# Taking the numerator of a linear-attention block two token tiles at a time, with other matmuls between it and the output projection

## The chip, the cores and the metric

The kernel runs on one core of a Trainium2 chip. Five engines work side by side and meet only at semaphores: TensorE (PE in the profile; PEld is its loading of weights), VectorE (DVE), ScalarE (ACT), GpSimd (POOL) and SyncE (SP), which issues most DMAs. Each engine takes its instructions strictly in the order in which they stand in its queue. The metric is the device time of one execution in microseconds (us).

## What is computed

One block of a network on 2048 tokens with 512 channels, in float32: linear attention with a learned feature map, then an MLP over the tokens.

```python
# attention, 32 heads of 16 channels, on the layer-normed x
phi_q = concat([softmax(pq), softmax(-pq)])     # pq = q @ w_phi, per head; phi_k likewise
kv  = einsum("bhsf,bhsd->bhfd", phi_k, v)
z   = einsum("bhsf->bhf", phi_k)
num = einsum("bhqf,bhfd->bhqd", phi_q, kv)
den = einsum("bhqf,bhf->bhq", phi_q, z) + 1e-6
h   = x + (num / den) @ wo
# token MLP on the layer-normed h
u   = gelu(einsum("bsd,sf->bdf", layernorm(h), w1) + b1)
out = h + (einsum("bdf,fs->bds", u, w2) + b2).transpose
```

## The kernel before, in words

The tokens lie in 16 tiles of 128. A first stage makes k, v and the sums kv and z. A second stage, the loop at L630, goes over the token tiles and makes num, the projection by wo, h and its normed copy. A last stage does the rest of the MLP: the matmuls with w1 that are still to do, gelu, and the matmuls with w2 (L764). Every large matmul is made of three: both factors are split into a high and a low part (`oh`/`ol`, `hs` with two halves, `whi`/`wlo`), and `mm3` (L60 to L64) adds high by high, high by low and low by high.

The loop of the second stage has 19 rounds, called `it`. What round `it` issues, by helper:

- `s_num(it-1)` (L536): 16 small matmuls, each on 64 rows and 32 columns of the array, give the numerator of one tile in PSUM (`tn`); ScalarE copies its high part to `oh` (L547), VectorE makes `ol` (`s_ol`, L552).
- `s_wo(it-2)` (L554): 12 matmuls of 512 columns into the one buffer `po`. VectorE then adds x (`s_h`, L568) and the result h goes out by DMA.
- `s_tr(it)` (L521): 8 transposes of the weighted features `eq` into `tn`, which has a single buffer of two PSUM banks and is shared with `s_num`; ScalarE copies them to `pht` (L527).
- `s_pq(it+1)` (L459, GpSimd): weights `eq` by one over the denominator. That comes from `s_ez` (L440, GpSimd, for tile it+3) and `s_den` (L444, VectorE, for tile it+2; its first step, L451, reduces `ez`).
- `s_moments(it-3)`, `s_rstd(it-3)`, `s_hn(it-3)` (L571 to L586): the layer norm of h on ScalarE and GpSimd. `s_hn` ends with the copy `hn` (ScalarE), the high part of `hs` (ScalarE, L57) and its low part (GpSimd, L58).
- Fills: `fill(p)` (L616) does 12 / 2 = 6 matmuls for one of the two column blocks of w1, p = 0 or p = 1, and one token tile whose `hs` is there. From round 6 on there are two of them in each round. The other fills, five more column blocks, follow after the loop. `fill_load` fetches the pieces of w1, ScalarE copies `whi` (L604), and `flush` (L593) makes `wlo` on VectorE (L596).

Inside the loop the order on PE, VectorE, ScalarE and GpSimd is the order of the program text: the loop stands in a manual schedule (L419) that is closed at L672. Behind it a scheduler orders the instructions. SyncE's queue is ordered by the scheduler throughout. Pools decide how many buffers a tile has; a new tile in a full pool waits until the old one was read for the last time.

Of the kernel before, what the change touches and what calls it, by code (L numbers as in the profile page):

```python
# [9 lines left out]
F32 = mybir.dt.float32  # L10
F32R = mybir.dt.float32r
AF = mybir.ActivationFunctionType
# [5 lines left out]
P = 128  # L18
S, D, H, DH, F = 2048, 512, 32, 16, 1792
NT = S // P  # L20
KD = D // P
NF = F // P
NG = 8
# [2 lines left out]
V_NOT = (0, 1, 11)  # L26
SUMS = 8
LAG = 4
WARM = 9
EPS = 1e-5  # L30

# [2 lines left out]
def block_kernel(ctx: ExitStack, tc: tile.TileContext, x, xT, wT, phic, wo, w1, b1, w2, b2,  # L34
                 kvmask, ident_in, out):
    nc = tc.nc
# [31 lines left out]
    ps_q = ctx.enter_context(tc.tile_pool(name="ps_q", bufs=2, space=PSUM, side="right"))  # L68
# [5 lines left out]
    kvB = wqp.tile([P, 2, P], F32, name="kvB")  # L74
# [87 lines left out]
    def turns(*lists):  # L162

        return [ops[i] for i in range(max(map(len, lists))) for ops in lists if i < len(ops)]

    def run(*lists):
        for op in turns(*lists):
            op()
# [4 lines left out]
    def heads(e):  # L173
        return e.rearrange("p g (a d) -> p (g a) d", d=DH)
# [43 lines left out]
    with tc.tile_pool(name="prep", bufs=1) as prep:  # L218
# [67 lines left out]
        warm = ps_k.tile([P, P], F32, name="pk_ps", tag="pk_ps")  # L286
        for _ in range(WARM):
            nc.tensor.matmul(warm, ones, ones, start=True, stop=True)
# [91 lines left out]
    def q_sums(lag):  # L380
        n = q["sum"]
        if n < min(NT, q["exp"] - lag + NT * (q["exp"] == NT)):
            q["sum"] += 1
            return q_sum(n)
        return []
# [54 lines left out]
    def s_ez(t):  # L440
        EZ[t] = az.tile([P, NG, P], F32, name="ez")
        nc.gpsimd.tensor_mul(EZ[t], EQ[t], zB)  # L442

    def s_den(t):  # L444


        tz = az.tile([P, NPR, 2, 2], F32, name="tz")
        den = az.tile([P, NPR, 2], F32, name="den")
        W[t] = az.tile([P, NPR, 2, 2], F32, name="w", bufs=3)
        other = SQ[t]  # L450
        return [lambda: nc.vector.reduce_sum(tz.rearrange("p g c h -> p (g c h)"), heads(EZ[t]), axis=AX.X),  # L451
                lambda: nc.vector.scalar_tensor_tensor(tz[:, :, 0], other[:, :, 1], 1e-6, tz[:, :, 0],
                                                       op0=ALU.mult, op1=ALU.add),
                lambda: nc.vector.tensor_mul(tz, other, tz),
                lambda: nc.vector.reduce_sum(den, tz.rearrange("p g c h -> p g h c"), axis=AX.X),
                lambda: nc.vector.reciprocal(den, den),
                lambda: nc.vector.tensor_mul(W[t], other, den.unsqueeze(2).to_broadcast([P, NPR, 2, 2]))]  # L457

    def s_pq(t):  # L459
        nc.gpsimd.tensor_mul(heads(EQ[t]), heads(EQ[t]), W[t].rearrange("p g c h -> p (g c h)").unsqueeze(2).to_broadcast([P, 2 * H, DH]))  # L460
# [51 lines left out]
    ps_f = ctx.enter_context(tc.tile_pool(name="ps_f", bufs=2, space=PSUM, reuse_waits="tile"))  # L512
# [3 lines left out]
    ak = a2.enter_context(tc.tile_pool(name="ak", bufs=2, reuse_waits="tile"))  # L516
    ps_t = a2.enter_context(tc.tile_pool(name="ps_t", bufs=1, space=PSUM, reuse_waits="tile"))
    ps_o = a2.enter_context(tc.tile_pool(name="ps_o", bufs=1, space=PSUM, reuse_waits="tile"))
    HN, HT, PHT, OS, PO, VE = {}, {}, {}, {}, {}, {}

    def s_tr(t):  # L521
        PHT[t] = ak.tile([P, NG, P], F32, name="pht")
        ptr = ps_t.tile([P, 2, 4, P], F32, name="tn")
        for g in range(NG):
            nc.tensor.transpose(ptr[:, g // 4, g % 4, :], EQ[t][:, g, :], ident)  # L525
        for half in range(2):
            nc.scalar.activation(PHT[t][:, half * 4:half * 4 + 4, :], ptr[:, half], AF.Copy)  # L527

    def s_kv():

# [2 lines left out]
            nc.tensor.transpose(pt[:, b, :], kvS[:, 2 * b:2 * b + 2, :].rearrange("p n f -> p (n f)"), ident)  # L533
        nc.scalar.activation(kvB, pt, AF.Copy)

    def s_num(t):  # L536

        pn = ps_t.tile([P, 2, 4, P], F32, name="tn")[:, :, 0:2]
        for b in range(2):
            for c in range(4):  # L540
                for r in range(2):
                    rows, cols = slice(64 * r, 64 * r + 64), slice(32 * c, 32 * c + 32)
                    nc.tensor.matmul(pn[cols, r, b, :], kvB[rows, b, cols], PHT[t][rows, 4 * b + c, :],  # L543
                                     start=True, stop=True, skip_group_check=True)
        oh = ak.tile([P, 2, 2, P], F32R, name="oh")
        ol = ak.tile([P, 2, 2, P], F32R, name="ol")
        nc.scalar.activation(oh, pn, AF.Copy)  # L547
        OS[t] = oh, ol, pn

    def s_ol(t):  # L550
        oh, ol, pn = OS[t]
        return [lambda: nc.vector.tensor_sub(ol, pn, oh)]  # L552

    def s_wo(t):  # L554
        oh, ol, _ = OS.pop(t)
        PO[t] = po = ps_o.tile([P, D], F32, name="po")
        for j in range(4):
            mm3(po, oh[:, j // 2, j % 2, :], ol[:, j // 2, j % 2, :], woh[:, j, :], wol[:, j, :], j == 0, j == 3)

    def s_x(t):  # L560
        HT[t] = ak.tile([P, D], F32, name="h", bufs=4)
        nc.sync.dma_start(HT[t], x[t * P:(t + 1) * P, :])

    def s_h(t):

        h = HT[t]
        VE[t] = ak.tile([P, 4], F32, name="ve2", bufs=3)
        nc.vector.scalar_tensor_tensor(h, PO.pop(t), 1.0, h, op0=ALU.mult, op1=ALU.add, accum_out=VE[t][:, 2:3])  # L568
        nc.sync.dma_start(out[t * P:(t + 1) * P, :], h)

    def s_moments(t):  # L571

        junk = ak.tile([P, D], F32, name="hj", bufs=1)
        nc.scalar.activation(VE[t][:, 1:2], VE[t][:, 2:3], AF.Copy, scale=-1.0 / D)
        nc.scalar.activation(junk, HT[t], AF.Square, bias=VE[t][:, 1:2], accum_out=VE[t][:, 3:4])
        nc.scalar.activation(VE[t][:, 0:1], VE[t][:, 3:4], AF.Identity, scale=(1.0 + EPS) / D, bias=eps2)

    def s_rstd(t):
        nc.gpsimd.tensor_tensor(r2[:, t:t + 1], VE[t][:, 0:1], mhalf[:, :1], op=ALU.pow)
        nc.gpsimd.tensor_mul(VE[t][:, 1:2], VE[t][:, 1:2], r2[:, t:t + 1])  # L580

    def s_hn(t):
        hn = ak.tile([P, D], F32, name="hn")
        nc.scalar.activation(hn, HT[t], AF.Identity, scale=r2[:, t:t + 1], bias=VE[t][:, 1:2])
        HN[t] = big.tile([P, 2, D], F32R, name="hs", tag="big")
        split(HN[t][:, 0], HN[t][:, 1], hn, nc.gpsimd)  # L586
# [4 lines left out]
    LATER = []  # L591

    def flush():  # L593
        while LATER:
            wl_, raw, wh_ = LATER.pop(0)
            LO.append(nc.vector.tensor_sub(wl_, raw, wh_).ins)  # L596
# [11 lines left out]
    PU, WI, LO = {}, {}, []  # L608
    FN, FL = [0] * (NF // 2), [0] * (NF // 2)

    def fill_load(p):
        if FL[p] < NT:
            WI[p, FL[p]] = stream(w1v, FL[p], 2, p * 256, 256)
            FL[p] += 2

    def fill(p, pool=None):  # L616

        t = FN[p]
        FN[p] = t + 1
        if FL[p] <= t:  # L620
            fill_load(p)
            flush()
        if t == 0:
            PU[p] = [pool.tile([P, D], F32, name="pu", tag="pu") for _ in range(2)]
        a, b = WI[p, t - t % 2]
        for c in range(2):
            mm3(PU[p][c], a[:, t % 2, c * P:(c + 1) * P], b[:, t % 2, c * P:(c + 1) * P],
                HN[t][:, 0], HN[t][:, 1], t == 0, t == NT - 1)

    for it in range(NT + 3):  # L630
        if 0 <= it < NT:
            s_x(it)
        if 0 <= it - 1 < NT:
            s_num(it - 1)
        if 0 <= it - 3 < NT:
            s_moments(it - 3)
        if 0 <= it - 2 < NT:
            s_wo(it - 2)
        if it == 1:
            run(q_logits(0))  # L640
            q_mm()
        if 0 <= it < NT:
            s_tr(it)
        if it == 0:
            s_kv()
        if 0 <= it + 1 < NT:
            s_pq(it + 1)
        if 0 <= it - 3 < NT:
            s_rstd(it - 3)
        lead(it, 1)  # L650
        den = s_den(it + 2) if it + 2 < NT else []
        ql = q_logits(1)
        ops = turns((s_ol(it - 1) if 0 <= it - 1 < NT else []) + ql + (q_sums(0) if it > 0 else []), den)

        at = 7 if ql else 3
        ops[at:at] = [flush]
        ops[3:3] = [lambda: s_h(it - 2)] if 0 <= it - 2 < NT else []
        run(ops)
        if it > 0:
            negate()  # L660
        if 0 <= it - 3 < NT:
            s_hn(it - 3)
        if FN[0] <= it - LAG:
            fill(0, ps_f)
        for _ in range(2):
            if q["logits"] == NT and FN[1] <= it - LAG:
                fill(1, ps_q)
        for p in range(2):
            if it >= LAG - 2 and FL[p] <= FN[p] + 1:
                fill_load(p)  # L670
    flush()
    ms.close()  # L672
# [102 lines left out]
    for n, (sp, p) in enumerate(STEPS):  # L775
        t = 2 * sp
# [93 lines left out]
```

## Time and profile before

| what | us |
|---|---|
| median of 3 timed runs | 530.6 |
| lowest, highest | 530.51, 530.87 |
| the profiled execution | 530.48 |
| its span, first to last instruction | 528.7 |
| start of the numerator of tile 0 (round 1), of tile 15 (round 16), from the span's start | 146.28, 256.88 |

A profile describes one execution. It gives each instruction's start and duration, and groups and merges them: a row of the timeline is start, duration, engine, line, operation, output and inputs, shape and how many were merged. Several matmuls are in flight at a time, so their durations overlap; the distance from one start to the next is what a matmul costs a full PE. L numbers are lines of the kernel before.

In the changed kernel, lines from L26 on stand at least one line lower.

### The profile page before, as it was taken

How to read it: one execution, taken by the hardware profiler on the slowest of the kernel's cores; microseconds unless marked ns; L12 is line 12 of the kernel's file. 1: busy time of each engine (PE TensorE's matmuls, PEld its weight loads, DVE VectorE, ACT ScalarE, POOL GpSimd, SP SyncE). 2: the span in 40 equal slices, each digit the busy share in tenths (PEclk: the TensorE clock that was granted, in tenths of full speed). 3: DMA queues.
4: the chain of work that ended last, by engine and by line, in shares of the span. 5: the costliest groups of instructions: out<-in, count | busy, mean ns of one | idle time of the engine just before them, and what ended most of it. 6: DMA issues, size and time to landing. Idle time of an engine off the chain costs nothing.

```text
span 528.7 us, 9887 instructions
## 1 busy us (share of the span) xinstructions
PE 521.3 (99%) x3872; PEld 450.0 (85%) x3872; DVE 378.8 (72%) x680; ACT 272.2 (51%) x460; POOL 230.9 (44%) x190
## 2 busy tenths in 40 slices
PE   8999999999999999999999999999999999999996
PEld 7888888887877777777888888888899999999996
DVE  6993999876899888773426424835668878987784
ACT  6998833525237776676657323526444243343340
POOL 2589699876999988985335000000001101101110
PEclk9999999999999999999999999999999999999999
DMA  8634300012303223333255333542015466535631
GB/s 315 199 116 119 90 33 21 1 45 97 102 1 100 73 89 119 121 121 120 81 178 161 104 97 98 161 119 81 20 41 113 134 152 151 128 122 121 160 73 48
DMA packets 45487, 55.85 MB, mean 106 GB/s; under 512 B 3968, under 2 KB 33024, under 8 KB 45440
## 3 DMA queue, kind: packets, MB, share of 16 engines
q1 hardware_dynamic: 43136, 51.38, 30.7%
q0 software_dynamic: 2016, 3.67, 5.2%
q8 instruction: 30, 0.49, 0.4%
q10 hardware_dynamic: 288, 0.17, 0.1%
q14 instruction: 17, 0.14, 0.1%
HBM read 46.81 MB, written 8.39 MB: 104 GB/s over the span
## 4 chain that ended last, share of the span: by engine, by line
PE 95%; DVE 3%; DMA 1%; ACT 0%; issue 0%; DVEq 0%
PE py L764 26%; PE pu L62 12%; PE pu L64 12%; PE pu L63 12%; PE po L62 3%; PE pv L63 3%; PE pv L64 3%; PE pv L62 3%; PE po L63 3%; PE po L64 3%; PE tn L525 3%; PE pk_ps L62 2%; PE pk_ps L64 2%; PE pk_ps L63 2%; PE tn L543 2%; PE kvp L207 2%
## 5 line engine op out<-in xcount | busy, mean ns | idle before, releaser
L802 POOL DMA_DIRECT2D out<-ot x14 | 12.5, 1000 | 211.9 <-DVE ot L800 211.9
L764 PE MATMUL py<-uf,whi 128*128 128x256 f32 x560 | 96.2, 283 | 0.0
L57 ACT ACTIVATE whi<-wraw 128x1792 fp32r<-128x1792 f32 x28 | 47.7, 1705 | 77.9 <-PE py L764 70.5
L62 PE MATMUL pu<-hs,whi 128*128 128x512 f32 x224 | 87.4, 393 | 0.0
L63 PE MATMUL pu<-hs,whi 128*128 128x512 f32 x224 | 87.2, 389 | 0.0
L64 PE MATMUL pu<-hs,wlo 128*128 128x512 f32 x224 | 87.0, 390 | 0.2 <-DVE wlo L596 0.2
L764 PEld LDWEIGHTS py<-uf,whi 128*128 128x128 f32 x560 | 83.3, 192 | 0.0
L596 DVE TENSOR_TENSOR wlo<-wraw,whi 128x512 fp32r<-128x512 f32 x56 | 45.1, 816 | 48.5 <-ACT whi L604 48.1
L764 PE MATMUL py<-uf,wlo 128*128 128x256 f32 x280 | 69.9, 283 | 0.0
L58 DVE TENSOR_TENSOR wlo<-wraw,whi 128x1792 fp32r<-128x1792 f32 x28 | 56.6, 2022 | 14.0 <-ACT whi L57 13.9
L604 ACT ACTIVATE whi<-wraw 128x512 fp32r<-128x512 f32 x56 | 34.4, 627 | 45.4 <-PE pu L63 41.4
L64 PEld LDWEIGHTS pu<-hs,wlo 128*128 128x128 f32 x224 | 42.0, 188 | 9.2 <-DVE wlo L596 0.6
L764 PEld LDWEIGHTS py<-uf,wlo 128*128 128x128 f32 x280 | 49.7, 192 | 0.0
L63 PEld LDWEIGHTS pu<-hs,whi 128*128 128x128 f32 x224 | 42.1, 188 | 8.4
L62 PEld LDWEIGHTS pu<-hs,whi 128*128 128x128 f32 x224 | 42.1, 188 | 8.4
L442 POOL TENSOR_TENSOR ez<-eq,zB 128x1024 f32<-128x1024 f32 x16 | 38.8, 2428 | 3.9 <-ACT zB L489 3.9
L764 PE MATMUL py<-un,whi 128*128 128x256 f32 x224 | 38.4, 283 | 0.0
L195 POOL TENSOR_TENSOR pk<-pk,sk 128x1024 f32<-128x1024 f32 x16 | 31.1, 1944 | 9.8 <-DVE sk L194 9.0
L527 ACT ACTIVATE pht<-tn 128x512 f32<-128x512 f32 x32 | 17.4, 596 | 33.4 <-PE tn L525 33.4
L764 PEld LDWEIGHTS py<-un,whi 128*128 128x128 f32 x224 | 33.2, 192 | 0.1
L460 POOL TENSOR_TENSOR eq<-eq,w 128x1024 f32<-128x1024 f32 x16 | 31.0, 1940 | 2.9 <-DVE w L457 2.9
L199 POOL TENSOR_TENSOR zacc<-zacc,pk 128x1024 f32<-128x1024 f32 x13 | 31.4, 2415 | 0.6
(165 smaller groups left out, 1185.3 us busy)
## 6 DMA issues: line engine op xcount, KB each, us to landing
wraw<-in_w SPq DMA_DIRECT2D x112, 256.0 KB, 2.9
xraw<-in_xT SPq DMA_DIRECT2D x16, 256.0 KB, 3.0
xh<-in_x SPq DMA_DIRECT2D x16, 256.0 KB, 2.7
h<-in_x SPq DMA_DIRECT2D x16, 256.0 KB, 3.5
out<-h SPq DMA_DIRECT2D x16, 256.0 KB, 2.0
out<-ot POOLq DMA_DIRECT2D x14, 256.0 KB, 4.6
wraw<-in_wT SPq DMA_DIRECT2D x12, 256.0 KB, 4.8
wo<-in_wo SPq DMA_DIRECT2D x4, 256.0 KB, 4.2
```

What stands on the lines that cost most here:

```text
L57: nc.scalar.activation(hi, src, AF.Copy)
L58: lo_engine.tensor_sub(lo, src, hi)
L62: nc.tensor.matmul(o, ah, bh, start=first, stop=False)
L63: nc.tensor.matmul(o, ah, bl, start=False, stop=False)
L64: nc.tensor.matmul(o, al, bh, start=False, stop=last)
L195: nc.gpsimd.tensor_mul(heads(PK[t]), heads(PK[t]), sk.unsqueeze(2).to_broadcast([P, 2 * H, DH]))
L199: nc.gpsimd.tensor_add(zacc, zacc, PK[t])
L442: nc.gpsimd.tensor_mul(EZ[t], EQ[t], zB)
L460: nc.gpsimd.tensor_mul(heads(EQ[t]), heads(EQ[t]), W[t].rearrange("p g c h -> p (g c h)").unsqueeze(2).to_broadcast([P, 2 * H, DH]))
L596: LO.append(nc.vector.tensor_sub(wl_, raw, wh_).ins)
L604: nc.scalar.activation(wh_, raw, AF.Copy)
L764: nc.tensor.matmul(o, a[x], b[:, y], start=start and i == 0, stop=stop and i == 2, skip_group_check=True)
```

## The change

The loop is cut in two. Rounds 0 to 9 are as before, except that tile 8's numerator, which stood in round 9, is left out of it. From round 10 on, even rounds take the numerators of two tiles at once (8 and 9 in round 10, then 10 and 11, 12 and 13, 14 and 15) with 256 columns for each small matmul. `pht` becomes one buffer for two tiles instead of two buffers for one each.

```diff
     def s_tr(t):
-        PHT[t] = ak.tile([P, NG, P], F32, name="pht")
+        j, i = divmod(t, 2)
+        if i == 0:
+            PHT[j] = ak.tile([P, NG, 2, P], F32, name="pht", bufs=1)
...
-    def s_num(t):
-        pn = ps_t.tile([P, 2, 4, P], F32, name="tn")[:, :, 0:2]
+    def s_num(t, n):
+        pn = ps_t.tile([P, 2, 2, 4 // 2, P], F32, name="tn")[:, :, :, 0:n]
...
-                    nc.tensor.matmul(pn[cols, r, b, :], kvB[rows, b, cols], PHT[t][rows, 4 * b + c, :],
+                    nc.tensor.matmul(pn[cols, r, b], kvB[rows, b, cols], PHT[t // 2][rows, 4 * b + c, t % 2:t % 2 + n],
...
-        nc.scalar.activation(oh, pn, AF.Copy)
-        OS[t] = oh, ol, pn
+        for i in range(n):
+            nc.scalar.activation(oh[:, i], pn[:, :, :, i], AF.Copy)
+            OS[t + i] = oh[:, i], ol[:, i], pn[:, :, :, i]
...
+    def two_fills(it, lag):
+        if FN[1] < it - lag:
+            fill(1, ps_q)
+        if FN[0] <= it - lag:
+            fill(0, ps_f)
...
+    for it in range(PAIRED + 2, NT + 3):
+        even = it % 2 == 0
+        if it + 1 < NT:
+            s_pq(it + 1)
+        if even and it <= NT:
+            s_num(it - 2, 2)
+        if even and it - 4 not in HN:
+            s_hn(it - 4)
+        den = s_den(it + 2) if it + 2 < NT else []
+        if even and it <= NT:
+            run(s_ol(it - 2) + den[:1] + s_ol(it - 1))
+            den = den[1:]
+        if it < NT:
+            s_x(it)
+        two_fills(it, LAG + (it > PAIRED + 2))
+        if even:
+            s_moments(it - 3)
+            if it - 2 < NT:
+                s_wo(it - 2)
+        if it < NT:
+            s_tr(it)
+        if not even:
+            if it - 2 < NT:
+                s_wo(it - 2)
+            s_moments(it - 3)
+        s_rstd(it - 3)
+        if it + 3 < NT:
+            s_ez(it + 3)
+        run(q_sums(0), den)
+        if not even:
+            flush()
+        if it - 2 < NT:
+            s_h(it - 2)
+        if even:
+            flush()
+            s_hn(it - 3)
+        for p in range(2):
+            if FL[p] <= FN[p] + 2:
+                fill_load(p)
```

On PE this gives the following order (numbers are token tiles; "fill p0 6" is the fill of column block 0 with tile 6).

| round | before | changed |
|---|---|---|
| 9 | num 8, wo 7, tr 9, fills p0 5, p1 5 | wo 7, tr 9, fills p0 5, p1 5 |
| 10 | num 9, wo 8, tr 10, fills p0 6, p1 6 | num 8+9, fill p0 6, wo 8, tr 10 |
| 11 | num 10, wo 9, tr 11, fills p0 7, p1 7 | tr 11, wo 9 |
| 12 | num 11, wo 10, tr 12, fills p0 8, p1 8 | num 10+11, fills p1 6, p0 7, wo 10, tr 12 |
| 13 | num 12, wo 11, tr 13, fills p0 9, p1 9 | fills p1 7, p0 8, tr 13, wo 11 |

The pattern of rounds 12 and 13 goes on to round 17. Three fills that stood in the loop come after it instead.

More of the change, by code (lines that the diff above doesn't have):

```diff
@@ L28 @@
 LAG = 4
+PAIRED = 8
 WARM = 9
@@ L526, in s_tr @@
         for half in range(2):
-            nc.scalar.activation(PHT[t][:, half * 4:half * 4 + 4, :], ptr[:, half], AF.Copy)
+            nc.scalar.activation(PHT[j][:, half * 4:half * 4 + 4, i, :], ptr[:, half], AF.Copy)
     def s_kv():
@@ L542, in s_num @@
                     rows, cols = slice(64 * r, 64 * r + 64), slice(32 * c, 32 * c + 32)
-                    nc.tensor.matmul(pn[cols, r, b, :], kvB[rows, b, cols], PHT[t][rows, 4 * b + c, :],
+                    nc.tensor.matmul(pn[cols, r, b], kvB[rows, b, cols], PHT[t // 2][rows, 4 * b + c, t % 2:t % 2 + n],
                                      start=True, stop=True, skip_group_check=True)
-        oh = ak.tile([P, 2, 2, P], F32R, name="oh")
-        ol = ak.tile([P, 2, 2, P], F32R, name="ol")
-        nc.scalar.activation(oh, pn, AF.Copy)
-        OS[t] = oh, ol, pn
+        oh, ol = [ak.tile([P, n, 2, 2, P], F32R, name=f"{name}{n}", bufs=3 - n) for name in ("oh", "ol")]
+        for i in range(n):
+            nc.scalar.activation(oh[:, i], pn[:, :, :, i], AF.Copy)
+            OS[t + i] = oh[:, i], ol[:, i], pn[:, :, :, i]
     def s_ol(t):
@@ L621, in fill @@
             fill_load(p)
+        if any(part is WI[p, t - t % 2][1] for part, _, _ in LATER):
             flush()
@@ L628, in fill @@
                 HN[t][:, 0], HN[t][:, 1], t == 0, t == NT - 1)
-    for it in range(NT + 3):
-        if 0 <= it < NT:
+    def two_fills(it, lag):
[3 more added lines that the diff above has]
+            fill(0, ps_f)
+    for it in range(PAIRED + 2):
+        if it < NT:
             s_x(it)
-        if 0 <= it - 1 < NT:
-            s_num(it - 1)
-        if 0 <= it - 3 < NT:
+        if 0 <= it - 1 < PAIRED:
+            s_num(it - 1, 1)
+        if it >= 3:
             s_moments(it - 3)
-        if 0 <= it - 2 < NT:
+        if it >= 2:
             s_wo(it - 2)
@@ L641, in block_kernel @@
             q_mm()
-        if 0 <= it < NT:
-            s_tr(it)
+        s_tr(it)
         if it == 0:
             s_kv()
-        if 0 <= it + 1 < NT:
-            s_pq(it + 1)
-        if 0 <= it - 3 < NT:
+        s_pq(it + 1)
+        if it >= 3:
             s_rstd(it - 3)
         lead(it, 1)
-        den = s_den(it + 2) if it + 2 < NT else []
         ql = q_logits(1)
-        ops = turns((s_ol(it - 1) if 0 <= it - 1 < NT else []) + ql + (q_sums(0) if it > 0 else []), den)
+        ops = turns((s_ol(it - 1) if 0 <= it - 1 < PAIRED else []) + ql + (q_sums(0) if it > 0 else []), s_den(it + 2))
         at = 7 if ql else 3
         ops[at:at] = [flush]
-        ops[3:3] = [lambda: s_h(it - 2)] if 0 <= it - 2 < NT else []
+        ops[3:3] = [lambda: s_h(it - 2)] if it >= 2 else []
         run(ops)
@@ L660, in block_kernel @@
             negate()
-        if 0 <= it - 3 < NT:
+        if it >= 3:
             s_hn(it - 3)
@@ L669, in block_kernel @@
             if it >= LAG - 2 and FL[p] <= FN[p] + 1:
+                fill_load(p)
+    for it in range(PAIRED + 2, NT + 3):
+        even = it % 2 == 0
+        if it + 1 < NT:
+            s_pq(it + 1)
+        if even and it <= NT:
[13 more added lines that the diff above has]
+                s_wo(it - 2)
+        if it < NT:
+            s_tr(it)
+        if not even:
[15 more added lines that the diff above has]
+            if FL[p] <= FN[p] + 2:
                 fill_load(p)
```

## The prediction

> **What bounds the kernel now.** I read the page first: busy time, the clock row, the chain that ended last.
>
> ```profile
> span 528.7 us, 9887 instructions
> PE 521.3 (99%) x3872; PEld 450.0 (85%) x3872; DVE 378.8 (72%) x680; ACT 272.2 (51%) x460; POOL 230.9 (44%) x190
> PEclk9999999999999999999999999999999999999999
> PE 95%; DVE 3%; DMA 1%; ACT 0%; issue 0%; DVEq 0%
> ```
>
> TensorE makes up 95% of the chain at an unthrottled clock. GpSimd's 44% is a mean over stages, so I asked for busy time in three rounds of the loop (columns: stretch, length, then PE, PEld, DVE, ACT, POOL).
>
> ```profile
> 206.80:213.96 7.16, 7.16 (x66) 5.66 (x65) 6.01 (x14) 5.00 (x11) 7.08 (x6) 1.00 0.32 103
> 213.96:221.11 7.15, 7.15 (x66) 5.65 (x65) 5.27 (x13) 4.40 (x10) 7.02 (x7) 1.00 0.36 119
> 242.57:249.72 7.15, 7.15 (x65) 5.66 (x64) 1.39 (x3) 4.40 (x10) 3.87 (x5) 1.00 0.36 117
> ```
>
> The stretches run from one numerator to the next, rounds 9, 10 and 14. PE is full in each and a round takes 7.15 us throughout. But in rounds 9 and 10, where the change begins, GpSimd is busy 7.08 and 7.02 us of it: nearly as full as PE. So two questions decide: what the change saves on PE, and whether the others still deliver in time for PE's new order.
>
> **What the change saves.** PE's timeline of round 9, then busy time in stretches of its numerator alone:
>
> ```profile
> 206.80 0.67 PE L543 MATMUL tn<-pht,kvB 64*32 64x128 f32 x32
> 207.40 0.50 PE L62 MATMUL po<-woh,oh 128*128 128x512 f32 x1
> 207.74 0.40 PE L63 MATMUL po<-wol,oh 128*128 128x512 f32 x1
> ...
> 210.02 0.39 PE L64 MATMUL po<-woh,ol 128*128 128x512 f32 x1
> 210.26 1.03 PE L525 MATMUL tn<-ident,eq 128*128 128x128 f32 x8
> 211.05 0.48 PE L62 MATMUL pu<-hs,whi 128*128 128x512 f32 x1
> 211.36 0.40 PE L63 MATMUL pu<-hs,whi 128*128 128x512 f32 x1
> ...
> 212.05 0.39 PE L63 MATMUL pu<-hs,whi 128*128 128x512 f32 x1
> 212.28 0.39 PE L64 MATMUL pu<-hs,wlo 128*128 128x512 f32 x1
> ...
> 213.64 0.39 PE L64 MATMUL pu<-hs,wlo 128*128 128x512 f32 x1
> 213.96 0.67 PE L543 MATMUL tn<-pht,kvB 64*32 64x128 f32 x32
> ```
> ```profile
> 206.80:206.93 0.13, 0.13 (x8) 0.13 (x16) 1.00 0.12 32
> 206.93:207.04 0.11, 0.11 (x16) 0.11 (x20) 1.00 0.00 0
> 207.04:207.15 0.11, 0.11 (x24) 0.11 (x16) 1.00 1.16 149
> ```
>
> A 512-column matmul costs 12.28 less 12.05, 0.23 us; twelve (wo, or two fills) cost 2.73. A numerator costs three things: 0.60 itself (207.40 less 206.80); 0.09 in front, as the last fill matmul holds PE for 0.32 (213.64 to 213.96) and not 0.23; and 0.11 behind, 0.34 (207.40 to 207.74) for 0.23. That is 0.80. The second fence cuts a numerator into stretches of its own: 8 new records in each, since 8 pieces of the array work side by side, and 0.11 us per group of 128 columns, four groups in all (32 records). With 256 columns a group has twice the columns to stream, so the second tile adds 4 x 0.107 = 0.43 (estimate; not in the trace). A pair costs 0.80 + 0.43 = 1.23 instead of 1.60: **0.37 saved, four times: 1.48**. From below I take 0.30 (the first group's 0.13 doubled too), from above 0.80, were the second tile free.
>
> A sentence that the rest can do without: the Trainium skill (TensorE: Matmul & The Clock Gate, "Back-to-back issue gap") gives N/2.4 + 2.5 ns, an estimate of 56 ns for 128 columns, by which a pair would save 0.58 and the whole come out 0.8 us lower; the row's 110 ns for these float32 records disagrees, and the measurement decides.
>
> Transposes 10 and 11 now stand one behind the other. A transpose block costs 0.08 behind it (211.05 to 211.36, 0.31 for 0.23) and 0.03 in front, once less: **0.11 saved**. The fills lose nothing: each still runs once, and three move behind the loop, where five further column blocks follow. The single `pht` buffer costs nothing: its new writer comes behind transposes that stand behind the last reading numerator on PE.
>
> **What it adds: three waits of PE in rounds 10 to 12.** Times are those of the trace, carried forward.
>
> ```profile
> 211.33 1.09 ACT L527 ACTIVATE pht<-tn 128x512 f32<-128x512 f32 x2 [1.88 <-PE tn L525]
> 213.15 0.64 ACT L57 ACTIVATE hs<-hn 128x512 fp32r<-128x512 f32 x1
> 214.73 0.60 ACT L547 ACTIVATE oh<-tn 128x512 fp32r<-128x512 f32 x1 [0.95 <-PE tn L543]
> ```
> ```profile
> 211.19 0.69 POOL L580 TENSOR_TENSOR ve<-ve,r 128x1 f32<-128x1 f32 x1
> 211.83 2.85 POOL L442 TENSOR_TENSOR ez<-eq,zB 128x1024 f32<-128x1024 f32 x1
> 214.64 1.30 POOL L58 TENSOR_TENSOR hs<-hn,hs 128x512 fp32r<-128x512 f32 x1
> 215.89 1.94 POOL L460 TENSOR_TENSOR eq<-eq,w 128x1024 f32<-128x1024 f32 x1
> 218.42 0.19 POOL L580 TENSOR_TENSOR ve<-ve,r 128x1 f32<-128x1 f32 x1
> 218.56 2.40 POOL L442 TENSOR_TENSOR ez<-eq,zB 128x1024 f32<-128x1024 f32 x1
> ```
> ```profile
> 211.14 1.29 DVE L596 TENSOR_TENSOR wlo<-wraw,whi 128x512 fp32r<-128x512 f32 x2
> 215.36 0.69 DVE L552 TENSOR_TENSOR ol<-tn,oh 128x512 fp32r<-128x512 f32 x1 [0.94 <-ACT oh L547]
> 215.97 1.21 DVE L451 TENSOR_REDUCE tz<-ez 128x64 f32<-128x1024 f32 x1
> ```
>
> *No wait of wo.* The longer way to `ol` lies under the fills that now stand between the numerator and wo: `oh` began 0.77 after its numerator (213.96 to 214.73), here 0.43 later, two copies take 1.1 and `ol` 0.69, so wo's third matmul could go 2.99 after the pair began; without the fills PE would want it at 1.6 and wait 1.4 in each pair.
>
> *First wait.* Without numerator 8, PE is 0.80 earlier: numerator 8+9 starts at 213.16. Its first fill matmul comes 0.60 + 0.43 later, at 214.19, the second at 214.53. The second needs the low half of `hs` of tile 6. Before, that fill stood behind wo and the transposes, at 218.2 (211.05 + 7.15); now it stands ahead of them. GpSimd finishes that half at 214.64 + 1.30 = 215.94, and its queue up to there is unchanged and full: **1.41 of waiting**. wo 8 and all of PE stand behind it. It could be shorter: two GpSimd rows before it are long (0.69 for 0.19, 2.85 for 2.40) beside VectorE's two `wlo`; undisturbed they give 0.95 back, leaving 0.46. If a `wlo` falls in less luckily, another 0.6: 2.0. I take the row as it is, since the same two `wlo` still come in round 9.
>
> *Second wait.* From 215.94 five more matmuls (1.14) and wo 8 (2.73) bring transpose 10 to about 219.85. Transpose 11 comes directly behind it into the same single `tn`, which ScalarE must first empty: in round 9 the copies end at 211.33 + 1.09 = 212.42, 2.16 after their transposes began (210.26), whereas the block holds PE for 0.79. **1.37 of waiting** for it and for wo 9 and numerator 10+11 behind it; at least that, up to 1.9 if ScalarE is late with its moments ahead of `pht` 10.
>
> *Third wait.* In round 12 VectorE's queue has `ol` 10, then the reduction of `ez` 14, then `ol` 11, for which transpose 12 waits. GpSimd, from 215.94: weighting and layer norm of tile 7 take 2.67 (215.89 to 218.56), `ez` 13 2.40, to 221.0. The low half of tile 7 waits for ScalarE, which has it ready 2.46 after its `pht` copy began (211.33 to 213.15 + 0.64), here 220.9 + 2.5 = 223.4; plus 1.30; plus 2.67; plus 2.40 for `ez` 14: 229.8, or 231.1 with two `wlo` in between. Reduction and `ol` add 1.21 + 0.69: 231.7 to 233.0. PE is at 222.0 with transpose 11, at 225.7 with numerator 10+11 (0.79 + 0.03 + 2.73 + 0.09), and would reach transpose 12 after 1.03 + 0.11, two fills and wo, at 232.3: 0 to 0.7, **I take 0.3**.
>
> From there on I see no further wait: two rounds take PE 1.23 + four times 2.73 + two transpose blocks of 0.90, 13.95 us for 14.3 before, and GpSimd, which has no `ez` after tile 15, gets ahead.
>
> ```profile
> 224.91 2.40 POOL L442 TENSOR_TENSOR ez<-eq,zB 128x1024 f32<-128x1024 f32 x1
> 225.45 3.01 DVE L596 TENSOR_TENSOR wlo<-wraw,whi 128x512 fp32r<-128x512 f32 x2
> ```
>
> Two `wlo` that take 1.29 elsewhere take 3.01 here; less the 1.86 for which `ez` still ran (to 227.31) they took 1.15. So one waits until the other is done. The Trainium skill (SBUF — State Buffer, "SBUF: two separate sides") says that GpSimd and a VectorE operation with two SBUF inputs lock one port pair against each other for a whole instruction; the trace agrees with these 3.01 us. By that rule the upper ends of the first and third wait are the likelier ones, and the sum would be 1.0 us higher.
>
> **Sum.** 1.41 + 1.37 + 0.3 = 3.08 added, 1.48 + 0.11 = 1.59 saved: +1.49. The profiled execution took 530.48 (its span 528.7 and 1.8 around it, unchanged), 0.1 under the median of 530.6: 530.48 + 1.49 = **532.0 us**. Lower end, shortest waits: 0.46 + 1.37 - 1.59 = +0.24. Upper end, longest waits and 0.30 per pair: 2.0 + 1.9 + 0.7 - 1.3 = +3.3. So 530.7 to 533.8.
>
> **Rivals.**
>
> *The waits are mostly covered* (530.7 us, no difference). GpSimd reaches tile 6 early, as the `wlo` fall into its idle time: only the second wait stays whole. For it: without `ol` 8, VectorE is earlier in round 9. Against it: GpSimd is busy 7.08 of 7.16 us there.
>
> *The second tile is free* (529.0 us, faster). If the array takes 256 columns in the time of 128 in these small pieces, each pair saves 0.80, in all 3.2 + 0.11, against waits of 0.46 + 1.37: -1.5. It decides from the point where the waits sum to less than 2.2. Against it: the even 0.11 per group.
>
> *GpSimd becomes the bound* (534.0 us). A GpSimd round is 6.3 undisturbed (214.64 to 218.56 + 2.40), 7.25 with the 0.95 of round 9; a changed PE round is 6.98. If each of the four rounds 10 to 13 waits for the 0.27, and the first and third wait are at 2.0 and 0.7, it is 1.1 + 2.0 + 1.4 + 0.7 - 1.59 = +3.6. Against it: tiles 7 to 9 are needed one to two rounds after they are made.
>
> **How the numbers follow.** Forecast 0.58, covered waits 0.19, free tile 0.13, GpSimd 0.10. A measurement of this kernel can tell about 0.2%, 1.06 us, from no change: 529.5 to 531.7. Of the forecast's ends, the part under 531.7 is about a fifth: slower 0.47 + 0.10 = 0.57; same 0.11 + 0.19 = 0.30; faster 0.13. The range runs from 529.7, which leaves out the free tile, to 533.8, the upper end of the forecast, which leaves out most of the GpSimd case.
>
> **What would show it.** Numerator rows with 256 columns, about 1.03 from their start to the next matmul; in round 10 a gap of 0.5 to 2 us before the second matmul of the fill, released by GpSimd's `hs`; a gap of about 1.4 between the two transpose blocks, released by the `pht` copy; a smaller one or none before transpose 12, from `ol`; from round 13 none. It is wrong if the first gap is missing, if pairs cost much less than 1.2, or if gaps appear in the later pairs or behind the loop.

## The result, and the profile after

The changed kernel takes **532.52 us**, the median of 6 runs (532.35 to 532.71); the kernel before takes 530.74 beside it (530.51 to 530.98, 6 runs). The ratio is 1.003, with a 95% interval of 1.002 to 1.0041: slower, by a little. The profiled execution took 532.35 and its span is 530.6, so 1.8 lies around the span, as before.

From the page of the changed kernel, the lines that answer to those of before:

```profile
span 530.6 us, 9637 instructions
PE 521.8 (98%) x3744; PEld 449.9 (85%) x3744; DVE 380.4 (72%) x680; ACT 272.1 (51%) x460; POOL 230.3 (43%) x190
PE 92%; DVE 3%; POOL 2%; ACT 2%; issue 0%; DVEq 0%; POOLq 0%
```

The profile has 128 matmul records fewer on TensorE (3872 to 3744: four numerators of 32 records each), and TensorE is still the chain. But the chain, 95% PE before, now runs 2% through GpSimd and 2% through ScalarE: in two places PE stands still until one of them has delivered. The view of PE's waits names them (columns: the waiting instruction, what released it, then us in total, times, longest).

```profile
PE tn L528 <- ACT pht L530: 1.2, 1, 1.2
...
PE pu L64 <- POOL hs L59: 0.8, 1, 0.8
```

Neither line is in the same view of the kernel before. PE's timeline of rounds 10 and 11 shows where they are (start, duration, engine, line, operation, output and inputs, shape, count; the bracket is the idle time in front and what ended it).

```profile
213.06 0.39 PE L65 MATMUL pu<-hs,wlo 128*128 128x512 f32 x1
213.38 1.09 PE L547 MATMUL tn<-pht,kvB 64*32 64x256 f32 x32
214.40 0.50 PE L63 MATMUL pu<-hs,whi 128*128 128x512 f32 x1
215.72 0.50 PE L64 MATMUL pu<-hs,whi 128*128 128x512 f32 x1 [0.81 <-POOL hs L59]
216.05 0.40 PE L65 MATMUL pu<-hs,wlo 128*128 128x512 f32 x1
...
219.78 1.03 PE L528 MATMUL tn<-ident,eq 128*128 128x128 f32 x8
222.04 1.06 PE L528 MATMUL tn<-ident,eq 128*128 128x128 f32 x8 [1.22 <-ACT pht L530]
222.86 0.48 PE L63 MATMUL po<-woh,oh 128*128 128x512 f32 x1
```

The paired numerator starts at 213.38 and holds PE for 1.02, to 214.40. There the first fill matmul starts, and the second comes 1.32 later, where 0.34 is usual behind a numerator: the first wait, 0.98. It costs 0.10 more, since the matmul that starts again from a standstill holds PE for 0.33 (215.72 to 216.05) and not 0.23: 1.08 in all. The block of transpose 10 begins at 219.78, holds PE for 0.79, and transpose 11 starts only at 222.04: the second wait, 2.26 - 0.79 = 1.47. The bracket shows less (0.81 and 1.22), because the row in front still counts as busy after the point where the next could have started (0.50 long, with 0.34 to the next start); the distance between starts is the cost.

The rows of the releasers, of GpSimd, VectorE and ScalarE in the changed kernel:

```profile
210.82 1.00 POOL L583 TENSOR_TENSOR r<-ve,mhalf 128x1 f32<-128x1 f32 x1
...
212.04 2.39 POOL L443 TENSOR_TENSOR ez<-eq,zB 128x1024 f32<-128x1024 f32 x1
214.39 1.27 POOL L59 TENSOR_TENSOR hs<-hn,hs 128x512 fp32r<-128x512 f32 x1
```
```profile
210.50 1.52 DVE L600 TENSOR_TENSOR wlo<-wraw,whi 128x512 fp32r<-128x512 f32 x2
...
230.21 1.22 DVE L452 TENSOR_REDUCE tz<-ez 128x64 f32<-128x1024 f32 x1 [1.26 <-POOL ez L443]
231.35 0.68 DVE L556 TENSOR_TENSOR ol<-tn,oh 128x512 fp32r<-128x512 f32 x1
```
```profile
220.86 1.08 ACT L530 ACTIVATE pht<-tn 128x512 f32<-128x512 f32 x2 [3.92 <-PE tn L528]
```

The low half of `hs` ends at 214.39 + 1.27 = 215.66 and PE goes on at 215.72. The `pht` copies end at 220.86 + 1.08 = 221.94 and transpose 11 starts at 222.04. The last two VectorE rows are for the third wait: `ol` 11 ends at 231.35 + 0.68 = 232.03. The same timeline, later on PE:

```profile
225.85 1.09 PE L547 MATMUL tn<-pht,kvB 64*32 64x256 f32 x32
...
232.54 1.03 PE L528 MATMUL tn<-ident,eq 128*128 128x128 f32 x8
...
239.93 1.09 PE L547 MATMUL tn<-pht,kvB 64*32 64x256 f32 x32
...
257.89 0.39 PE L63 MATMUL po<-woh,oh 128*128 128x512 f32 x1
...
260.70 0.40 PE L63 MATMUL pu<-hs,whi 128*128 128x512 f32 x1
```

Transpose 12 starts at 232.54 with no bracket, half a microsecond after `ol` 11 was there: the third wait is missing. From 225.85 to 239.93 two rounds take 14.08 us, for 14.3 before, and without any wait. So every pair gains, but less than forecast: 13.95 had been worked out. Where the missing 0.13 is shows in the last two rows: wo takes 2.81 (260.70 less 257.89). In the kernel before the corresponding wo, between two fills, takes 2.72:

```profile
263.04 0.39 PE L62 MATMUL po<-woh,oh 128*128 128x512 f32 x1
...
265.76 0.39 PE L62 MATMUL pu<-hs,whi 128*128 128x512 f32 x1
```

Nothing about wo was changed in number, shape or order of its matmuls. It is 12 matmuls at 0.234 instead of 0.227. What did change is where its stationary operand lies: `oh` and `ol` were rewritten for two tiles, and in the compiled kernel they lie at byte 147552 and 151648 of a partition, each 96 past a multiple of 2048; before, they lie on multiples of 2048 (133120 and 137216, for instance). The experiments test whether that is the cause.

**Where the time went.** The stage in question lasts from the first transpose to the first matmul with w2. Rows of the kernel before, then of the changed one:

```profile
142.25 1.09 PE L525 MATMUL tn<-ident,eq 128*128 128x128 f32 x8
...
382.72 0.40 PE L764 MATMUL py<-un,whi 128*128 128x256 f32 x2
```
```profile
142.50 1.09 PE L528 MATMUL tn<-ident,eq 128*128 128x128 f32 x8
...
384.57 0.40 PE L812 MATMUL py<-un,whi 128*128 128x256 f32 x2
```

240.47 us became 242.07: **+1.60**. The parts read off above: first wait +1.08, second +1.47, third 0, pairs -1.52 (four times 1.60 - 1.22, the 1.22 being 1.02 for the numerator, 0.09 in front and 0.11 behind), one transposes' transition -0.11, and eight wo of about 0.08 each, +0.66. Together +1.58.

### The profile page after: what moved, and what is told of

It reads as the page before. It is cut to its first block, busy times and chain, and to the rows that moved or that the text cites. A ratio compares the mean times of both kernels' runs of the same rounds, so it can differ in the third digit from the quotient of the medians.

```text
span 530.6 us, 9637 instructions
## 1 busy us (share of the span) xinstructions
PE 521.8 (98%) x3744; PEld 449.9 (85%) x3744; DVE 380.4 (72%) x680; ACT 272.1 (51%) x460; POOL 230.3 (43%) x190
## 4 chain that ended last, share of the span: by engine, by line
PE 92%; DVE 3%; POOL 2%; ACT 2%; issue 0%; DVEq 0%; POOLq 0%
PE py L812 26%; PE pu L63 12%; PE pu L64 12%; PE pu L65 12%; PE pv L64 3%; PE pv L65 3%; PE pv L63 3%; PE pk_ps L63 2%; PE po L63 2%; PE pk_ps L64 2%; PE pk_ps L65 2%; PE po L65 2%; PE po L64 2%; PE tn L528 2%; PE kvp L208 2%; PE tn L547 1%
## 5 line engine op out<-in xcount | busy, mean ns | idle before, releaser
L600 DVE TENSOR_TENSOR wlo<-wraw,whi 128x512 fp32r<-128x512 f32 x56 | 46.4, 837 | 51.4 <-ACT whi L608 51.1
```

## The experiments

The theory: the pairing saves what it should on PE, two waits of PE in rounds 10 and 11 take more than that, for want of independent matmuls there, and the address of `oh` and `ol` costs the rest. The rivals: the slower wo comes from something other than the address (traffic of the other engines, the longer numerator); GpSimd is the bound, so that a wait removed in round 10 comes back later; the fills are short in these rounds, so that a fill that covers one wait uncovers another.

The first stage of all these kernels is the same code, and yet its end moves by up to 1 us between executions (first transpose from 142.22 to 143.27). So the effects are read from the stage length, between those two rows, and the ratios of the timed runs stand beside it. All that follows is in this table (us; times are medians, the kernel before was timed beside each; "change" is the stage less 240.47).

| kernel | time (runs) | before beside it | ratio, 95% interval | first transpose | first w2 matmul | change |
|---|---|---|---|---|---|---|
| changed kernel | 532.52 (6) | 530.74 | 1.003 [1.002, 1.0041] | 142.50 | 384.57 | +1.60 |
| 1 changed, aligned | 532.26 (12) | 531.08 | 1.0018 [1.0009, 1.0027] | 143.27 | 384.70 | +0.96 |
| 2 before, moved 96 bytes | 532.10 (12) | 531.08 | 1.0018 [1.0009, 1.0027] | 143.01 | 384.50 | +1.02 |
| 3 changed, low half on VectorE | 532.15 (12) | 531.08 | 1.0019 [1.001, 1.0029] | 142.41 | 383.81 | +0.93 |
| 4 changed, fill between | 532.35 (12) | 531.08 | 1.0021 [1.0012, 1.0031] | 142.90 | 384.65 | +1.28 |
| 5 refilled, aligned, from 8 | 529.91 (11) | 531.07 | 0.9983 [0.9974, 0.9992] | 142.80 | 382.30 | -0.97 |
| 6 the same from 6 | 530.22 (11) | 531.07 | 0.9981 [0.9972, 0.999] | 143.20 | 382.86 | -0.81 |
| 7 the same from 10 | 530.40 (11) | 531.07 | 0.9996 [0.9987, 1.0005] | 143.06 | 382.72 | -0.81 |
| 8 wo ahead of the fills | 536.99 (3) | 531.07 | 1.0114 [1.0098, 1.013] | 142.22 | 388.98 | +6.29 |
| 9 before, moved 64 bytes | 531.61 (1) | 531.02 (1) | none | 142.53 | 383.88 | +0.88 |
| 10 before, moved 128 bytes | 531.46 (1) | 531.02 (1) | none | 142.38 | 383.70 | +0.85 |

### 1. The changed kernel, with `oh` and `ol` back on the grid

An unused tile ahead of the second loop moves the pair's `oh` and `ol` to 149504 and 153600, multiples of 2048.

```diff
+    ak.tile([P, 488], F32, name="pad", bufs=1)
     for it in range(PAIRED + 2, NT + 3):
```

> The changed kernel with a pad of 1952 bytes in front of the pair buffers of oh and ol, so that they start at a multiple of 2048 bytes again (now 96 bytes past one). In the changed kernel a wo from round 10 on takes 2.81 us to the next block where it took 2.72 before. Theory: the weights' address costs it, 7 ns per matmul, so eight wo give back 8 x 0.09 = 0.7 us: 531.8, with wo blocks of 2.72 to 2.73. Rival: the pitch comes from the neighbours (copies on ScalarE and VectorE beside wo in the new order), then 532.5 and 2.81 as now.

The last wo of the loop, in PE's timeline of this kernel:

```profile
258.22 0.39 PE L63 MATMUL po<-woh,oh 128*128 128x512 f32 x1
...
260.94 0.39 PE L63 MATMUL pu<-hs,whi 128*128 128x512 f32 x1
```

It takes 2.72 again, and the stage is 0.64 shorter than the changed kernel's (+0.96 for +1.60); two later rounds take 13.91. The two waits are whole (1.2 and 0.8 in the view of waits, as in the changed kernel). So the address accounts for 0.64, near the 0.66 read off above, and for nothing of the waits. Against the kernel before on its chip the time is +1.18, where the changed kernel's was +1.78: the same 0.6.

### 2. The kernel before, with `oh` and `ol` moved off the grid

```diff
+        if t == 0:
+            ak.tile([P, 24], F32, name="pad", bufs=1)
         oh = ak.tile([P, 2, 2, P], F32R, name="oh")
```

> The kernel before, order and sizes untouched, with a pad of 96 bytes in front of its oh and ol. Theory (address): all sixteen wo slow down by 0.06 to 0.09 us, 531.7 to 532.1, and a wo between two fills takes 2.81 instead of 2.72. Rival (neighbours): 530.7 and 2.72.

Its last wo, in PE's timeline:

```profile
264.72 0.39 PE L62 MATMUL po<-woh,oh 128*128 128x512 f32 x1
...
267.53 0.40 PE L62 MATMUL pu<-hs,whi 128*128 128x512 f32 x1
```

2.81, in a kernel without pairs and without the new order. The stage grows by 1.02. The rows of the sixteen wo hold 0.80 of it, 0.05 each; the other 0.22 lies in the fills and numerators beside them and is not explained. Traffic of the new order and the longer numerator are ruled out as the cause, as this kernel has neither. The pad also moves the layer norm's tiles behind `ol`, which TensorE does not read; in run 1 `oh` and `ol` alone move.

### 3. The low half of tile 6 on VectorE

This leaves everything but one instruction: the low half of `hs` of tile 6, on which the first wait depends, is made by VectorE, which stands idle then.

```diff
-        split(HN[t][:, 0], HN[t][:, 1], hn, nc.gpsimd)
+        split(HN[t][:, 0], HN[t][:, 1], hn, nc.vector if t == PAIRED - 2 else nc.gpsimd)
```

> The changed kernel with one operation on another engine: the low half of hs of tile 6, for which the fill in round 10 waits 1.1 us, is made by VectorE, which idles there, and not at the end of GpSimd's queue. Theory (PE's waits add up): the first wait goes, the others stay, 532.5 - 1.0 = 531.5. Rival (GpSimd as a whole bounds rounds 10 to 13): what PE gains in round 10 it waits for in rounds 11 to 13, 532.2 to 532.5.

PE, GpSimd and VectorE around it in this kernel:

```profile
214.34 0.50 PE L63 MATMUL pu<-hs,whi 128*128 128x512 f32 x1
214.95 0.50 PE L64 MATMUL pu<-hs,whi 128*128 128x512 f32 x1
```
```profile
211.95 2.39 POOL L443 TENSOR_TENSOR ez<-eq,zB 128x1024 f32<-128x1024 f32 x1
214.31 2.39 POOL L461 TENSOR_TENSOR eq<-eq,w 128x1024 f32<-128x1024 f32 x1
```
```profile
213.56 1.34 DVE L59 TENSOR_TENSOR hs<-hn,hs 128x512 fp32r<-128x512 f32 x1 [0.36 <-ACT hs L58]
```

The first wait shrinks from 0.98 to 0.27 (0.61 less the usual 0.34), and the stage by 0.67, so nearly all of what is gained in round 10 stays gained: no later wait takes it back. This speaks against GpSimd as the bound, but not alone, since the edit also takes an instruction off GpSimd; run 5 leaves GpSimd its work. The wait does not go altogether, because VectorE's copy takes 1.34 instead of some 0.65 (half of two `wlo` at 1.29): it begins at 213.56 while `ez` holds GpSimd until 214.34, and ends at 214.90, 0.56 after it. In turn the weighting behind it on GpSimd takes 2.39 instead of 1.94. The Trainium skill (SBUF — State Buffer, "SBUF: two separate sides") says that GpSimd and a VectorE operation with two SBUF inputs exclude each other for a whole instruction; these rows agree with it.

### 4. A fill between the two transposes

```diff
+        if it == PAIRED + 3:
+            fill(1, ps_q)
         if it < NT:
             s_tr(it)
```

> The changed kernel with the fill of column block 1 and tile 6 moved from round 12 to between transposes 10 and 11. Theory, additive: the second wait of 1.4 us goes, 531.1. Rival: round 12 then has one fill between its numerators and wo, and wo 10 waits for ol 10 behind two wlo and h on VectorE and for GpSimd's ez 14, 1 to 1.5 us given back, 532.0 to 532.4. The replayed queues speak for the rival.

PE's timeline of this kernel:

```profile
220.17 1.03 PE L528 MATMUL tn<-ident,eq 128*128 128x128 f32 x8
220.96 0.48 PE L63 MATMUL pu<-hs,whi 128*128 128x512 f32 x1
...
222.43 1.06 PE L528 MATMUL tn<-ident,eq 128*128 128x128 f32 x8
...
231.60 0.39 PE L65 MATMUL po<-woh,ol 128*128 128x512 f32 x1
232.55 1.06 PE L528 MATMUL tn<-ident,eq 128*128 128x128 f32 x8 [0.56 <-DVE tz L453]
```

Transpose 11 follows the fill with no wait: the second wait is gone, 1.47 us of standing still replaced by 1.47 us of work. But the stage shortens by 0.32 only. The fill that now stands in round 11 is one of the two that stood between the pair 10+11 and wo 10 in round 12. With one fill there, wo 10 comes sooner and takes 3.68 up to transpose 12 (228.87 to 232.55) instead of 2.81, with a wait of 0.7 in front of the transposes where the changed kernel has none: the forecast's third wait, which appears as soon as round 12 has less to do. (The bracket names the VectorE instruction right behind `ol` 11; `ol` 11 itself runs from 231.72 to 232.40.) Added up, the second wait's 1.47 less 0.87 for wo 10 and 0.11 for the transition between the two transposes, which is no longer saved, leaves 0.49 against the 0.32 measured. Of the 0.17 between them 0.12 stands in front of wo 10, whose first matmul starts 0.35 after the fill's last one and not 0.23 (VectorE reads `po` of wo 9 until 228.72); the rest is not placed. The time, 532.35, is the rival's (532.0 to 532.4) and not the additive 531.1. So the waits hang together: what is short in rounds 10 to 12 is work that PE could do meanwhile.

### 5. The same fills, placed otherwise

In the changed kernel two fills stand in round 9, where nothing waits. One of them is taken from there.

```diff
-            if q["logits"] == NT and FN[1] <= it - LAG:
+            if q["logits"] == NT and FN[1] <= it - LAG and it <= PAIRED:
                 fill(1, ps_q)
...
+    ak.tile([P, 488], F32, name="pad", bufs=1)
     for it in range(PAIRED + 2, NT + 3):
...
-        two_fills(it, LAG + (it > PAIRED + 2))
+        if it == PAIRED + 2:
+            fill(1, ps_q)
+        elif it > PAIRED + 3:
+            two_fills(it, LAG + 1)
...
+        if it == PAIRED + 3:
+            fill(0, ps_f)
         if it < NT:
             s_tr(it)
```

So the fill of block 1 with tile 5 covers the copies of the pair 8+9, and the fill of block 0 with tile 6 covers those of transpose 10. `oh` and `ol` are on the grid.

> Aligned buffers, and the same thirteen fills up to round 11 in other places: the fill p1 5 leaves round 9 and stands between numerator 8+9 and wo 8, and p0 6 stands between transposes 10 and 11. Theory (PE lacked the right fill at the right place): first and second wait both go, about 2.4 us, on top of the 0.7 for the address; what is left is the saving of the four pairs. The stage is 1.3 to 1.6 us shorter than before and the median lies near 529.6, faster than both kernels. Rival (GpSimd and VectorE bound rounds 10 to 13): the waits come back before transpose 12 or in the fill with tile 8, 530.7 to 532.

PE's timeline of this kernel:

```profile
212.34 1.09 PE L547 MATMUL tn<-pht,kvB 64*32 64x256 f32 x32
213.37 0.50 PE L63 MATMUL pu<-hs,whi 128*128 128x512 f32 x1
...
215.09 0.39 PE L64 MATMUL po<-wol,oh 128*128 128x512 f32 x1
215.68 0.50 PE L65 MATMUL po<-woh,ol 128*128 128x512 f32 x1 [0.21 <-DVE ol L556]
...
218.88 0.48 PE L63 MATMUL pu<-hs,whi 128*128 128x512 f32 x1
...
220.34 1.06 PE L528 MATMUL tn<-ident,eq 128*128 128x128 f32 x8
```

The first wait and the second are gone. What is left is one of 0.5: wo 8's third matmul waits for `ol` (215.68 less 215.09 is 0.59 for 0.23, and 0.10 for starting again), since one fill is 1.4 us of cover and the copies take longer. Four pairs at -0.38 and 0.5 make -1.02; the stage says -0.97, less than the 1.3 to 1.6 that were expected without that wait. The time is 0.9983 of the kernel before, with an interval of 0.9974 to 0.9992: faster than both kernels, by a little, with the same matmuls as the changed one.

### 6 and 7. The same from the sixth and from the tenth tile

```diff
-PAIRED = 8
+PAIRED = 6
```

and 10 instead of 6 in run 7.

> As the run before, pairs from tile 6 on: five pairs. Theory: a fifth saving of 0.37 less a wait of wo 6 for its oh and ol in round 8, where ScalarE still makes exponentials and VectorE is fullest, 0 to 1.2: stage 0.9 to 1.9 shorter than the kernel before, median 529.2 to 530.2. Rival: 530.7 or more, as VectorE and GpSimd cannot follow.

> As the run before but one, pairs from tile 10 on: three pairs. If what counts is the number of pairs times 0.37 and no wait is left, the stage is 1.0 to 1.2 shorter than before and the median near 530.0. If rounds 10 to 13 of the four-pair version still hold waits, this one is faster than it.

A fifth pair does not add its 0.38. In run 6 the view of waits has

```profile
PE po L65 <- DVE ol L556: 0.5, 1, 0.5
```

for 0.2 in run 5. Wo 6 takes 3.63 instead of 2.73, and its first matmul comes 1.73 after the fill in front of it began, for 1.49 in run 5: 1.14 of waiting. ScalarE begins `oh` 2.13 after the numerator (198.34 to 200.47) and in run 5 1.49 (212.34 to 213.83), and `ol` is later by as much. In both the layer norm's two copies come first; in run 6 an exponential of 1.15 still stands ahead of them (at 198.04). Five pairs at -0.38 and 1.14 make -0.76, and the stage gains 0.81 instead of 0.97. With three pairs the wait shrinks to 0.25 (wo 10 takes 2.97), and the stage also gains 0.81: one pair less, a quarter of a microsecond less waiting. Both stay under what was expected (0.9 to 1.9 and 1.0 to 1.2). The timed runs of run 7 are not clear of no change (0.9987 to 1.0005). Between 5, 6 and 7 the stages differ by 0.16, and the intervals overlap; which of them is best is open.

### 8. wo directly behind the pair

The fills of the even rounds go behind wo instead of ahead of it; `oh` and `ol` are on the grid.

```diff
-        two_fills(it, LAG + (it > PAIRED + 2))
         if even:
             s_moments(it - 3)
             if it - 2 < NT:
                 s_wo(it - 2)
+        two_fills(it, LAG + (it > PAIRED + 2))
```

> The changed kernel, aligned, with one part taken away: in even rounds wo stands directly behind the numerators and the fills behind wo. Theory: wo's first matmul then waits for oh and its third for ol, together about 1.4 us in each of four pairs, while the fill of tile 6 comes late enough for GpSimd; the second wait stays. 532.3 + 4 x 1.4 - 1.1 = 536.8. Rival: the fills are not needed as cover, 531 to 532.5.

The view of PE's waits in this kernel, then PE's timeline of round 10:

```profile
PE po L63 <- ACT oh L551: 2.3, 3, 0.8
PE po L63 <- DVE h L572: 1.5, 1, 1.5
PE po L65 <- DVE ol L556: 1.4, 3, 0.5
```
```profile
213.12 1.09 PE L547 MATMUL tn<-pht,kvB 64*32 64x256 f32 x32
214.97 0.50 PE L63 MATMUL po<-woh,oh 128*128 128x512 f32 x1 [0.76 <-ACT oh L551]
215.30 0.40 PE L64 MATMUL po<-wol,oh 128*128 128x512 f32 x1
216.18 0.50 PE L65 MATMUL po<-woh,ol 128*128 128x512 f32 x1 [0.48 <-DVE ol L556]
```

The prediction had wo's third matmul 2.99 after the pair began and 1.4 of waiting in each pair; it comes 3.06 after (213.12 to 216.18). By the distances between starts, wo begins 1.85 after the numerator instead of 1.02, its third matmul comes 0.88 after the second instead of 0.23, and 0.10 goes for starting again: 1.58 a pair, alike in three of the pairs. In the fourth, wo 10 begins 2.63 after the numerator (225.95 to 228.58), 1.61 more than usual: it waits for the one buffer `po`, which `s_h` of wo 9 reads only after two `wlo` that take 3.02 us. The stage is 6.29 longer than before, 5.33 longer than that of run 1, from which it differs only in this order. Three times 1.58 and 1.61 make 6.35; the first wait, which is gone here, takes 1.08 off: 5.27 of the 5.33. Without the fills as cover a pair costs four times what it saves.

### 9 and 10. How far off the grid

The edit of run 2 with `[P, 16]` and `[P, 32]`: 64 and 128 bytes past the multiples of 2048.

> The kernel before with its oh and ol 64 bytes past a multiple of 2048 (96 in an earlier run). One look at wo's blocks. If any address off the 2048 grid costs, a wo between two fills takes 2.76 to 2.81 us and the stage is about 1 us longer; if a smaller grid of 64 bytes or less is what counts, 2.72 and no change.

> The same with 128 bytes. If the grid that counts is 128 bytes or less, 2.72 and the stage as before; otherwise 2.76 to 2.81.

The last wo takes 2.80 and 2.79 in them, 2.81 with 96 bytes, 2.72 with none, and the stages grow by 0.88 and 0.85. So 64 and 128 bytes cost nearly what 96 do. A multiple of 2048 is not needed, though: the stationary operand of one matmul is a quarter of the tile, 512 bytes, so with the tile on the multiple three of four quarters begin 512, 1024 or 1536 past it, and all twelve matmuls of wo still take 0.227. If a grid is what counts, its step is more than 128 bytes and at most 512; nothing between was tried.

## Why the prediction was right, step by step

**The direction and the mechanism** held: slower, because PE waits in round 10 for GpSimd's half of tile 6 and between transposes 10 and 11 for ScalarE's copy, and these take more than four pairs save.

**The saving per pair** was forecast at 0.37 and is 0.38: the second tile costs 0.42 (1.02 for 0.60) where 0.43 was worked out from the even 0.11 per group. That rules the free second tile out. The formula that the Trainium skill gives (TensorE: Matmul & The Clock Gate, "Back-to-back issue gap") had led to an estimate of 0.58; the measured 0.38 decides.

**The transposes' transition**, 0.11: consistent with the sum, not measured by itself.

**The first wait** was put at 1.41, up to 2.0, and is 1.08. The step took GpSimd's rows of before as they were, "since the same two `wlo` still come in round 9". They come, but earlier: VectorE, which has no `ol` 8 in that round, runs them at 210.50 instead of 211.14, and 0.25 earlier still when counted from the stage's start. There they lie beside the layer norm's small rows on GpSimd (one takes 1.00, elsewhere 0.55) and no longer beside `ez`, which takes its undisturbed 2.39 instead of 2.85. The half is ready at 215.66, before at 215.94, which is 0.53 earlier when counted from the stage's start. The prediction had this as the argument of a rival and let the full queue of GpSimd outweigh it. That the lock made the upper end likelier was wrong with it.

**The second wait** was put at 1.37 and is 1.47: the copies end 2.16 after the transposes began, to the hundredth, and another 0.10 goes by from there until transpose 11 starts.

**The third wait** was put at 0.3, 0 to 0.7, and is 0: `ol` 11 is there at 232.03, PE at 232.54. Run 4 brought it out by taking a fill away from round 12, so the chain of reasons (reduction of `ez` 14 ahead of `ol` 11) was right and only its size was off by 0.8: 0.3 short was forecast, 0.5 to spare was measured.

**No wait of wo** held, and run 8 shows the price of it.

**GpSimd as the bound** is ruled out by the later rounds without a wait and by run 5, where GpSimd has the same work and the stage is shorter than before; run 3 points the same way. **Mostly covered waits** is ruled out by the two rows in PE's list.

**What was missing.** The terms that were forecast sum to 1.08 + 1.47 - 1.52 - 0.11 = +0.92 by measurement, and run 1, which has only these, has +0.96. The prediction had +1.49 and the stage +1.60. So the sum came out near in part by chance: the forecast held 0.33 too much in the first wait and 0.3 in the third, against 0.1 too little in the second, and the surplus was replaced by 0.66 that no step held. With the two tiles of the pair on the grid the kernel would still have been slower, at 1.0018 [1.0009, 1.0027], so the sign does not hang on it.

**Where the expected gain went.** Four pairs gave the 1.5 us they promised; the two waits at the seam between the two loops, where the fills run out for a round, took it, and an address took more. Run 5 has the same matmuls and keeps 1.0 of the 1.5.

## What to carry to other kernels

When a reordering makes TensorE faster, list for each of its new neighbours what the other engines must finish in between, and count the independent matmuls that are at hand to cover it: here a gain of 0.38 a pair was lost to 2.55 us of waits in two rounds, and moving one fill out of a round where nothing waited, and another to between the transposes, won most of it back. A cover that is moved to one wait uncovers another (run 4), so all of the rounds around the seam have to be laid out together. When a tile's shape changes, look at where the allocator puts it and compare the distance between matmuls on instructions that were not touched.

## What the runs showed of the hardware that was not expected

- A matmul of 512 columns whose stationary operand lies in a tile 64, 96 or 128 bytes past a multiple of 2048 takes 0.233 to 0.234 us in a full stream, for 0.227 with the tile on the multiple: 2.79 to 2.81 for the twelve of wo, for 2.72 (runs 9, 2, 10; undone in run 1). With the tile on the multiple, operands that begin 512, 1024 and 1536 bytes past it take 0.227 as well. Whether it is `oh`, `ol` or both that matter was not told apart, nor why: what the runs show is the address and the price.
- A matmul of 512 columns that starts again behind a wait holds TensorE for 0.33 to 0.34 and not 0.23 (215.72 to 216.05 in the changed kernel, 0.33 in run 5), so such a wait costs 0.10 more than the standing still itself. In one case, wo 10 in run 8, it was 0.30.
- The same code ahead of the stage ends between 142.22 and 143.27 in the twelve traces: a spread of 1 us, as large as the effects that were looked for. The differences of stage lengths, each from one trace, agree with those of the medians to 0.2 us in the runs with 6 to 12 executions, and to 0.4 in runs 8, 9 and 10.
